# A fused attention and two-expert-stage kernel: 64-bit weight words decoded two tiles at a time, and the first chunk's last four feature blocks computed with split operands

## The chip, the cores and the metric

The kernel runs on one core of one Trainium2 chip. The metric is the device time of one execution in microseconds, the median of three runs.

## What is computed

Three stages follow each other. Windowed attention (4 batches, 8 heads, 576 positions, window 64) gives 2304 rows of 512 numbers. A dense two-layer stage (512 to 2048 to 512) follows, and then a routed stage with 8 experts, where each row goes to one of them. The change touches the dense stage and what is around its start:

```
x = attn_out.transpose(0, 2, 1, 3).reshape(B * S, H * D)     # 2304 x 512
h = x @ w_in                                                 # 512 x 2048
g = where(h >= 1, h, where(h <= -1, 0, (h + 1) ** 2 / 4))
y = g @ w_out                                                # 2048 x 512
# then: expert = argmax(y @ w_gate + bias), out = gate * (relu(y @ w1[e]) @ w2[e])
```

The arrays w_in and w_out reach the device as 64-bit floating-point words, and the kernel turns them into 32-bit numbers itself.

## The kernel before

The rows are worked through in 6 chunks of 384. Within a chunk the loop runs over 16 feature blocks f of 128 columns. For each block, layer 1 (`l1`) multiplies the chunk's x with the block of w_in into a PSUM tile h, ScalarE makes u from it (L456 and L457), VectorE finishes the activation (`act2`, L465), and two steps later (`LAG`) layer 2 (`l2`) multiplies it with the block of w_out and adds into three PSUM tiles py. There are two PSUM tiles h, so `l1` of block f+1 can start only when `act2` of block f-1 has read its h.

TensorE has two ways of doing a product here. With whole 32-bit operands it is 4 matmuls for layer 1 (L436, each recorded as two instructions) and 3 for layer 2 (L483). With split operands, each number is a rounded high part plus a low part, and high times high, high times low and low times high are added: 12 matmuls for layer 1 (L453), 9 for layer 2 (L491). Splitting a weight tile takes a copy on ScalarE (L301) and a subtraction on VectorE (L302). Splitting an activation takes a copy on ScalarE (L473) and a subtraction on VectorE (L474).

In chunk 0 the weights arrive and are decoded step by step, and both layers work on whole operands. A weight tile is [128, 512], and tiles come in pairs p: pair p holds block p-1 of w_out and block p+1 of w_in. Each tile of a pair passes through four kinds of operation: ScalarE takes the magnitude of the upper words (`dec_abs`, L258), VectorE clamps and shifts (`dec_clamp`, L265 and L267), and VectorE merges sign and lower word (`dec_merge`, L273 and L278). In step f, pair f+1 is clamped and merged and pair f+2 gets its magnitudes. Each instruction handles one tile, 512 columns wide, and the two tiles of a pair take turns.

From chunk 1 on, both layers use split operands. The 32 weight tiles are split from the end of chunk 0 into the first half of chunk 1 (`split`). Small copies on GpSimd (`hold_back`, L292) keep the target tiles from being written too early.

The attention of the rows of chunk 1 runs inside the steps of chunk 0: score products on TensorE (L331), the row maximum on VectorE (L346), the exponential on ScalarE (L356), the sum's reciprocal on VectorE (L368, L369), the scaling on ScalarE (L377), the transpose on TensorE (L386), its copy (L391), the product with v (L408) and its split into xh and xl (L428, L429). In chunk 0 every engine's instructions are issued in the order in which `step0` writes them, each engine working strictly through its own row. In chunk 1 a scheduler mixes the engines' rows.

Of the kernel before, what the change touches and what calls it, by code (L numbers as in the profile page):

```python
# [9 lines left out]
F32 = mybir.dt.float32  # L10
F32R = mybir.dt.float32r
# [6 lines left out]
P = 128  # L18
# [53 lines left out]
def moe_kernel(ctx, tc, qT, kT, v, w_in, w_out, mod, wg, wgT, mbias, w1, w2, cst, tri, empty, out, spec):  # L72
# [129 lines left out]
    dec = tile_of([P, 4 * 2 * DM], "dec", I32)  # L202

    PRE = 3

    def part(kind, f, lo):
        return parts[kind, f][0][:, lo * WB : (lo + 1) * WB]

    def raw_home(p, u):
        j = 2 * p + u  # L210
        if j == 2 * NF - 1:
            return dts[p][u]
        if j // 2 not in raws:
# [15 lines left out]
    pairs += [((1, f), (0, f + IN0 - 2)) for f in range(2, NF - IN0 + 2)]  # L229
    pairs += [((1, f), (1, f + 1)) for f in range(NF - IN0 + 2, NF, 2)]  # L230
    NPR = len(pairs)
    dts = {}
# [11 lines left out]
    def words(p, u):  # L244
        w = raw(p, u).rearrange("p (n w) -> p n w", w=2)
        return w[:, :, 0], w[:, :, 1]

    def dec_load(p, us=(0, 1)):
        if p < NPR:
# [3 lines left out]

    def dec_abs(p, us=(0, 1)):
        if p < NPR:
            for u in us:
                dts.setdefault(p, {})[u] = tile_of([P, DM], f"dt{p}_{u}", I32, tag="y", bufs=4)
                A.activation(dts[p][u].bitcast(F32), words(p, u)[1].bitcast(F32), AF.Abs)  # L258

    def dec_clamp(p, us=(0, 1)):  # L260
        if p < NPR:
            t = dts[p]
            for u in us:
                tf = t[u].bitcast(F32)
                V.tensor_scalar(tf, tf, c0, c1, op0=ALU.max, op1=ALU.min)  # L265
            for u in us:
                V.tensor_scalar(t[u], t[u], 5, 2, op0=ALU.logical_shift_left, op1=ALU.logical_shift_right)  # L267

    def dec_merge(p, us=(0, 1)):
        if p < NPR:  # L270
            t = dts[p]
            for u in us:
                V.scalar_tensor_tensor(  # L273
                    t[u], words(p, u)[1], -0x40000000, t[u], op0=ALU.bitwise_and, op1=ALU.bitwise_or
                )
            for u in us:
                w = raw_home(p, u)
                V.scalar_tensor_tensor(  # L278
                    w, words(p, u)[0], 29, t[u], op0=ALU.logical_shift_right, op1=ALU.bitwise_or
                )  # L280
                whole[pairs[p][u]] = w.bitcast(F32)

    whole = {}
    splits = [kf for p in pairs for kf in p]

    def home(k):
        return f"T{NF + k if k < NF else k - NF}"

    def hold_back(g):
        for k in range(len(parts), NF):  # L290
            t = tile_of([P, 2 * WB], f"hold{k}", tag=home(k))
            G.tensor_copy(t[:, :1], g[:, :1])  # L292

# [12 lines left out]

    def new_x(c):
        if c == 0:
            xs[c] = tile_of([P, KD, CT], "x0", tag="xh", bufs=2)
            return  # L310
        xs[c] = tuple(tile_of([P, KD, CT], f"x{s}{c}", F32R, tag=f"x{s}", bufs=2) for s in "hl")

    at, xos = {}, {}
    PAIRED = 2 * BPC
# [102 lines left out]
    def att_x(i):  # L417
        xo = xos.pop(i)
        c, n = divmod(i, BPC)
        dst = slice(n * BLK, (n + 1) * BLK)  # L420
        if i >= PAIRED:
            xos.pop(i + 1)
            dst = slice(n * BLK, n * BLK + GT)
        if c == 0:
            A.copy(xs[c][:, :, dst], xo)
# [7 lines left out]
    def l1_whole(f, g):  # L433
        h = hs[0, f]
        for k in range(KD):
            T.matmul(h[:, g], whole[0, f][:, k * P : (k + 1) * P], xs[0][:, k, g], start=k == 0, stop=k == KD - 1)  # L436

    def l1_tile(t):
        if t == 0:
# [3 lines left out]
    def l1(c, f):  # L443
        if (c, f) not in hs:
            hs[c, f] = ps.tile([P, CT], F32, tag="h", name=f"h{c}_{f}", bufs=2)
            if c == 0:
                l1_whole(f, slice(0, CT))
        h = hs[c, f]
        n = 0
        xh, xl = xs[c] if c else (None, None)  # L450
        for k in range(KD if c else 0):
            for a, b in ((0, xh), (0, xl), (1, xh)):
                T.matmul(h, wi(f, a)[:, k, :], b[:, k, :], start=n == 0, stop=n == 3 * KD - 1)  # L453
                n += 1
        u = tile_of([P, CT], f"u{c}_{f}", tag="u", bufs=2)
        A.activation(u, h, AF.Relu, bias=half, scale=0.5)  # L456
        A.activation(u, u, AF.Square)  # L457
        us[c, f] = u

    def act2(c, f):  # L460
        u, h = us[c, f], hs.pop((c, f))
        g = u
        if c == 0:
            g = gs[c, f] = tile_of([P, CT], f"g{c}_{f}", tag="gh" if f % 2 else "gl", bufs=2)
        V.scalar_tensor_tensor(g, u, 1.0, h, op0=ALU.min, op1=ALU.max)  # L465

    def gsplit(c, f):
        u = us.pop((c, f))
        if c == 0:
            return  # L470
        gh = tile_of([P, CT], f"gh{c}_{f}", F32R, tag="gh", bufs=2)
        gl = tile_of([P, CT], f"gl{c}_{f}", F32R, tag="gl", bufs=2)
        A.copy(gh, u)  # L473
        V.tensor_tensor(gl, u, gh.bitcast(F32), op=ALU.subtract)  # L474
        gs[c, f] = (gh, gl)

    def l2(c, f):
        if f == 0:
            ys[c] = [ps.tile([P, DM], F32, tag=f"y{t}", name=f"py{c}_{t}", bufs=1) for t in range(TT)]
        if c == 0:  # L480
# [491 lines left out]
    def step0(f):  # L972
        if 1 <= f < 4:
            act2(0, f - 1)
        dec_clamp(f + 1)
        dec_merge(f + 1)
        dec_load(f + 4)
        if f >= NF - 2:
            split(2 if f < NF - 1 else 6)
        at_step = {f - st: BPC + k for k, st in enumerate(FIRST)}  # L980
        if 4 in at_step:
            att_pv(at_step[4])
            att_x(at_step[4])
# [175 lines left out]
```

## Time and profile before

| | |
|---|---|
| median of 3 runs | 738.86 us (738.45 to 739.05) |
| the profiled execution, device time | 737.79 us |
| its span, first to last instruction | 736.1 us |
| mean granted TensorE clock | 0.997 of full speed |
| TensorE matmul busy | 723.4 us, 98% |
| VectorE busy | 470.0 us, 64% |
| ScalarE busy | 385.1 us, 52% |
| GpSimd busy | 127.0 us, 17% |

The share of busy time is a mean over stages. Chunk 0 of the dense stage runs from about 20 to 120 us, and chunk 1 from 113 to about 195 us. A matmul's duration in a row includes the time that it spends in the pipeline, so the time from one group of matmuls to the next is read from their starts.

### The profile page before, as it was taken

The numbers are of one execution on the slowest core, as the hardware profiler recorded it, in microseconds if no ns is written. First come the engines' busy times: TensorE is split into PE (matmuls) and PEld (weight loads), VectorE is DVE, ScalarE is ACT, GpSimd is POOL, SyncE is SP. The second block draws the span as 40 slices with busy tenths as digits, with TensorE's granted clock in tenths as the row PEclk, the third lists the DMA queues.
The fourth block names the chain that finished last, engine by engine and source line by source line (L and its number), as shares of the span: only waits on it lengthen the run. The fifth ranks groups of instructions, "written<-read, shape, count | busy, mean of one in ns | idle before, by whom it ended". The sixth has DMA issues, their size and how long they took to land. (4 is left out here: it accounts for less than half of the span.)

```text
span 736.1 us, 12397 instructions
## 1 busy us (share of the span) xinstructions
PE 723.4 (98%) x4168; PEld 617.6 (84%) x4168; DVE 470.0 (64%) x1430; ACT 385.1 (52%) x933; POOL 127.0 (17%) x189
## 2 busy tenths in 40 slices
PE   8999999999999999999999999999999999999995
PEld 6655556888988989898998899899989989898984
DVE  5998889984387528962596638866674554453500
ACT  6775679654455546554555445645434544443511
POOL 3200002012001201120111412032048222201010
PEclk9999999999999999999999999999999999999998
DMA  9986633220022203220310005145456654445300
GB/s 327 334 305 222 245 120 127 91 61 28 32 92 65 80 15 107 73 81 15 108 58 30 2 27 186 60 93 192 161 127 179 220 183 153 158 160 165 119 32 19
DMA packets 48570, 89.26 MB, mean 121 GB/s; under 512 B 6976, under 2 KB 16320, under 8 KB 48368
## 3 DMA queue, kind: packets, MB, share of 16 engines
q1 hardware_dynamic: 44064, 78.36, 32.0%
q0 software_dynamic: 4288, 9.79, 4.9%
q8 instruction: 35, 0.57, 0.3%
q14 instruction: 39, 0.32, 0.1%
q10 hardware_dynamic: 144, 0.22, 0.1%
HBM read 78.89 MB, written 9.87 MB: 121 GB/s over the span
## 5 line engine op out<-in xcount | busy, mean ns | idle before, releaser
L453 PE MATMUL h<-xh,w 128*128 128x384 f32 x640 | 180.0, 342 | 0.4 <-DVE u L465 0.4
L491 PE MATMUL py<-w,gh 128*128 128x512 f32 x480 | 148.6, 393 | 0.0
L453 PEld LDWEIGHTS h<-xh,w 128*128 128x128 f32 x640 | 117.1, 188 | 3.4 <-DVE u L465 0.7
L453 PE MATMUL h<-xl,w 128*128 128x384 f32 x320 | 107.4, 336 | 0.0
L456 ACT ACTIVATE u<-h,half 128x384 f32<-128x384 f32 x96 | 55.4, 577 | 94.6 <-PE h L453 70.8
L737 DVE TENSOR_TENSOR e<-wr,e 128x512 fp32r<-128x512 f32 x112 | 74.6, 689 | 45.3 <-ACT e L736 43.3
L799 PE MATMUL hp<-zh,e 128*128 128x384 f32 x384 | 101.1, 336 | 0.1
L491 PEld LDWEIGHTS py<-w,gh 128*128 128x128 f32 x480 | 88.7, 188 | 14.6
L814 PE MATMUL yo<-e,hm 128*128 128x512 f32 x348 | 99.0, 395 | 0.0
L491 PE MATMUL py<-w,gl 128*128 128x512 f32 x240 | 94.0, 397 | 0.0
L465 DVE SCALAR_TENSOR_TENSOR u<-u,h 128x384 f32<-128x384 f32 x80 | 44.0, 550 | 74.0 <-ACT u L457 73.7
L545 DVE CUSTOM_DVE_ANT_0 prod<-y,wgb 128x512 f32<-128x512 f32 x120 | 85.1, 709 | 1.2
L473 ACT CAST gh<-u 128x384 fp32r<-128x384 f32 x80 | 41.1, 513 | 73.2 <-PE py L491 29.7
L814 PEld LDWEIGHTS yo<-e,hm 128*128 128x128 f32 x348 | 64.2, 188 | 12.4
L736 ACT CAST e<-wr 128x512 fp32r<-128x512 f32 x112 | 66.2, 616 | 16.2 <-DMA wr<-in_w 16.0
L799 PEld LDWEIGHTS hp<-zh,e 128*128 128x128 f32 x384 | 69.7, 188 | 1.3 <-DVE hm L802 0.6
L379 POOL TENSOR_TENSOR s<-s,sm 128x512 f32<-128x512 f32 (+1 forms) x24 | 26.3, 1096 | 234.0 <-DVE sm L369 166.9
L799 PE MATMUL hp<-zl,e 128*128 128x384 f32 x192 | 64.3, 335 | 0.0
L453 PEld LDWEIGHTS h<-xl,w 128*128 128x128 f32 x320 | 60.2, 188 | 2.3 <-issue 0.2
L474 DVE TENSOR_TENSOR gl<-u,gh 128x384 fp32r<-128x384 f32 x80 | 44.9, 561 | 26.9 <-ACT gh L473 26.1
L491 PEld LDWEIGHTS py<-w,gl 128*128 128x128 f32 x240 | 44.8, 188 | 9.5
L356 ACT ACTIVATE s<-s,mx 128x128 f32<-128x128 f32 (+1 forms) x120 | 45.9, 384 | 13.1 <-DVE mx L346 13.1
(209 smaller groups left out, 1054.8 us busy)
## 6 DMA issues: line engine op xcount, KB each, us to landing
wr<-in_w SPq DMA_DIRECT2D x112, 256.0 KB, 2.9
q<-in_qT SPq DMA_DIRECT2D x32, 256.0 KB, 3.6
dec<-in_w_in SPq DMA_DIRECT2D x16, 512.0 KB, 5.2
dec<-in_w_out SPq DMA_DIRECT2D x16, 512.0 KB, 4.0
v<-in_v SPq DMA_DIRECT2D x27, 256.0 KB, 2.9
k<-in_kT SPq DMA_DIRECT2D x15, 384.0 KB, 4.7
yd<-y SPq DMA_DIRECT2D x18, 256.0 KB, 2.2
wgb<-in_wgT SPq DMA_DIRECT2D x1, 2048.0 KB, 7.4
```

The source lines that it names most:

```text
L356: A.activation(s[:, hp, :n], s[:, hp, :n], AF.Exp, bias=mx[:, hp : hp + 1], scale=-1.0, accum_out=sm[:, hp : hp + 1],)
L453: T.matmul(h, wi(f, a)[:, k, :], b[:, k, :], start=n == 0, stop=n == 3 * KD - 1)
L456: A.activation(u, h, AF.Relu, bias=half, scale=0.5)
L465: V.scalar_tensor_tensor(g, u, 1.0, h, op0=ALU.min, op1=ALU.max)
L473: A.copy(gh, u)
L474: V.tensor_tensor(gl, u, gh.bitcast(F32), op=ALU.subtract)
L491: T.matmul(ys[c][t], a[:, sl], wo(f, b), start=f == 0 and n == 0, stop=f == NF - 1 and n == 2)
L545: V.tensor_tensor_reduce(prod, yt[t], wgb[0][:, e, :], 1.0, 0.0, ALU.mult, ALU.add, lg[:, t, e : e + 1])
L736: A.copy(wpart(i, p, 0), t)
L737: V.tensor_tensor(wpart(i, p, 1), t, wpart(i, p, 0).bitcast(F32), op=ALU.subtract)
L799: T.matmul(hp, w1s(i, f, k, a), b[:, k, :], start=n == 0, stop=n == 3 * KD - 1)
L814: T.matmul(yo, a[f][:, sl], w2s(i, f, b), start=n == 0, stop=n == 3 * NF2 - 1)
```

## The change

Two things are changed.

First, the decoding handles both tiles of a pair with one instruction where the pair's words lie next to each other (two pairs of three): magnitudes, clamp, shift and merges are then 1024 columns wide. In the third pair of three only clamp and shift are. The pair's intermediate tile moves from four half-size buffers into two full-size ones.

Second, the blocks 12 to 15 of chunk 0 use split operands in layer 1 and in layer 2. For this, x of chunk 0 is split in two halves (`split_x0`, in steps 8 and 9), the weight tiles concerned are split within steps 11 to 15 (`split_hi` at the end of a step on ScalarE, `split_lo` at the start of the next on VectorE, ahead of that step's decoding), and the activations of blocks 12 to 15 are split (`gsplit`, called in `step0` ahead of `dec_abs`). The number of weight splits stays 32: ten lie in chunk 0, 22 in chunk 1.

```diff
+    soon = {f: [(0, f + 1)] for f in range(FS1 - 1, NF - 1)}
+    for f in range(FS2, NF - 1):
+        soon.setdefault(f + 1, []).append((1, f))
+    soon[NF - 1] += [(0, 0), (0, 1), (1, NF - 1)]
...
     def dec_clamp(p, us=(0, 1)):
         if p < NPR:
-            t = dts[p]
-            for u in us:
-                tf = t[u].bitcast(F32)
-                V.tensor_scalar(tf, tf, c0, c1, op0=ALU.max, op1=ALU.min)
-            for u in us:
-                V.tensor_scalar(t[u], t[u], 5, 2, op0=ALU.logical_shift_left, op1=ALU.logical_shift_right)
+            t = dts[p][:, us[0] : us[-1] + 1]
+            V.tensor_scalar(t.bitcast(F32), t.bitcast(F32), c0, c1, op0=ALU.max, op1=ALU.min)
+            V.tensor_scalar(t, t, 5, 2, op0=ALU.logical_shift_left, op1=ALU.logical_shift_right)
...
+    def split_hi(kf):
+        tag = free.pop(0)
+        t = tile_of([P, 2 * WB], f"w{kf[0]}_{kf[1]}", F32R, tag=tag)
+        w = whole.pop(kf)
+        A.copy(t[:, :WB], w)
+        halves.append((kf, t, tag, w))
+
+    def split_lo():
+        kf, t, tag, w = halves.pop(0)
+        V.tensor_tensor(t[:, WB:], w, t[:, :WB].bitcast(F32), op=ALU.subtract)
...
     def step0(f):
         if 1 <= f < 4:
             act2(0, f - 1)
+        if f == NF - 1:
+            free.extend(f"T{NF + k}" for k in (14, 15, 8, 9))
+        for kf in soon.get(f, []):
+            split_lo()
         dec_clamp(f + 1)
         dec_merge(f + 1)
         dec_load(f + 4)
-        if f >= NF - 2:
-            split(2 if f < NF - 1 else 6)
+        if f in (FS1 - 4, FS1 - 3):
+            split_x0(f - FS1 + 4)
...
         l1(0, f)
         if f >= 4:
             act2(0, f - 1)
+            gsplit(0, f - 1)
+        else:
+            us.pop((0, f - 1), None)
         dec_abs(f + 2)
...
         if f >= LAG:
             l2(0, f - LAG)
+        for kf in soon.get(f + 1, []):
+            split_hi(kf)
```

Where the instructions stand now is shown at three places. The first is VectorE at step 12 of chunk 0, before. dt13 is the intermediate of pair 13, raw13 its decoded tiles, g0_11 the finished activation of block 11, sm11 the sum of an attention block.

```order
L265 TENSOR_SCALAR dt13_0_979<-dt13_0_979 128x512
L265 TENSOR_SCALAR dt13_1_981<-dt13_1_981 128x512
L267 TENSOR_SCALAR dt13_0_979<-dt13_0_979 128x512
L267 TENSOR_SCALAR dt13_1_981<-dt13_1_981 128x512
L273 SCALAR_TENSOR_TENSOR dt13_0_979<-dec_106,dt13_0_979 128x512
L273 SCALAR_TENSOR_TENSOR dt13_1_981<-dec_106,dt13_1_981 128x512
L278 SCALAR_TENSOR_TENSOR raw13_1003<-dec_106,dt13_0_979 128x512
L278 SCALAR_TENSOR_TENSOR raw13_1003<-dec_106,dt13_1_981 128x512
L465 SCALAR_TENSOR_TENSOR g0_11_1021<-u0_11_974,h0_11_969 128x384
```

The same place on VectorE now; w0_13 is the split tile of block 13 of w_in.

```order
L320 TENSOR_TENSOR w0_13_946<-raw12_893,w0_13_946 128x512
L274 TENSOR_SCALAR dt13_930<-dt13_930 128x1024
L275 TENSOR_SCALAR dt13_930<-dt13_930 128x1024
L281 SCALAR_TENSOR_TENSOR dt13_930<-dec_106,dt13_930 128x1024
L294 SCALAR_TENSOR_TENSOR raw13_951<-dec_106,dt13_930 128x1024
L508 SCALAR_TENSOR_TENSOR g0_11_977<-u0_11_925,h0_11_920 128x384
```

Eight instructions of 512 columns have become four of 1024, each working on what the one ahead of it wrote, and the weight's low part stands ahead of all of them.

The second place is ScalarE at the end of step 11, before. u0_11 is block 11's activation, s11 an attention block, ts10 a copied transpose.

```order
L456 ACTIVATE u0_11_974<-h0_11_969,half_78 128x384
L457 ACTIVATE u0_11_974<-u0_11_974 128x384
L258 ACTIVATE dt13_0_979<-dec_106 128x512
L258 ACTIVATE dt13_1_981<-dec_106 128x512
L356 ACTIVATE s11_983,sm11_989<-s11_983,mx11_984 128x128 x4
L391 COPY ts10_1011<-pt10_1006 128x512
```

The same place on ScalarE now.

```order
L499 ACTIVATE u0_11_925<-h0_11_920,half_78 128x384
L500 ACTIVATE u0_11_925<-u0_11_925 128x384
L269 ACTIVATE dt13_930<-dec_106 128x1024
L398 ACTIVATE s11_932,sm11_938<-s11_932,mx11_933 128x128 x4
L315 CAST w0_13_946<-raw12_893 128x512
L433 COPY ts10_959<-pt10_954 128x512
```

The copy that VectorE's first instruction of step 12 works on stands behind the four exponentials.

The third place is ScalarE in steps 12 to 14, now: the scaling of s11 (which uses the reciprocal sm11 that VectorE computes behind g0_11), and the activation's high part gh0_12.

```order
L269 ACTIVATE dt14_979<-dec14_1_858 128x512
L419 ACTIVATE s11_932<-s11_932,sm11_938 128x128 x4
L315 CAST w0_14_991<-raw13_951 128x512
L315 CAST w1_12_993<-raw13_951 128x512
L470 CAST xh1_424<-xo10_1004 128x4x64
L499 ACTIVATE u0_13_1028<-h0_13_1015,half_78 128x384
L500 ACTIVATE u0_13_1028<-u0_13_1028 128x384
L516 CAST gh0_12_1032<-u0_12_974 128x384
L269 ACTIVATE dt15_1036<-dec_106 128x1024
L315 CAST w0_15_1041<-raw14_999 128x512
L315 CAST w1_13_1043<-raw14_999 128x512
```

Before, the same stretch holds the scaling, the activations and the two magnitudes of dt15, without the five copies L315 and L516.

```order
L258 ACTIVATE dt14_1_1025<-dec14_1_906 128x512
L377 ACTIVATE s11_983<-s11_983,sm11_989 128x128 x4
L428 CAST xh1_427<-xo10_1045 128x4x64
L456 ACTIVATE u0_13_1061<-h0_13_1056,half_78 128x384
L457 ACTIVATE u0_13_1061<-u0_13_1061 128x384
L258 ACTIVATE dt15_0_1066<-dec_106 128x512
L258 ACTIVATE dt15_1_1068<-dec_106 128x512
```

The copies of the weights now stand behind the scaling in one step, and behind gh0_12 and the magnitudes in the next.

## Rows read from the trace of the kernel before

**Rows 1.** Busy time of each engine in one stretch: PE, PEld, DVE, ACT, POOL, clock, DMA.

```profile
100.00:120.00 20.00, 20.00 (x95) 13.17 (x94) 19.73 (x49) 16.88 (x39) 2.55 (x8) 1.00 0.50 178
```

**Rows 2.** TensorE's timeline in chunk 0: start, duration, line, operation, tiles, count.

```profile
82.34 1.16 PE L331 MATMUL sc<-k,q 128*128 128x128 f32 x8
...
85.92 2.74 PE L483 MATMUL py<-raw,g 128*128 128x512 f32 x6
88.50 0.60 PE L386 MATMUL pt<-cs,s 128*128 128x128 f32 x4
88.93 2.75 PE L436 MATMUL h<-x,raw 128*128 128x384 f32 x8
91.52 2.74 PE L483 MATMUL py<-raw,g 128*128 128x512 f32 x6
94.18 0.69 PE L408 MATMUL xo<-ts,v 128*64 128x64 f32 x16
94.80 2.85 PE L436 MATMUL h<-x,raw 128*128 128x384 f32 x8
```

**Rows 3.** VectorE's timeline in steps 11 and 12 of chunk 0.

```profile
85.78 0.28 DVE L346 CUSTOM_DVE_ANT_0 s<-sc,cs 128x128 f32<-128x128 f32 x1
...
87.85 1.00 DVE L265 TENSOR_SCALAR dt<-dt 128x512 f32<-128x512 f32 x2 [1.15 <-ACT dt L258]
...
89.44 1.28 DVE L273 SCALAR_TENSOR_TENSOR dt<-dec,dt 128x512 int32<-128x512 int32 x2
...
91.85 0.54 DVE L465 SCALAR_TENSOR_TENSOR g<-u,h 128x384 f32<-128x384 f32 x1
...
92.50 0.18 DVE L369 RECIPROCAL sm<-sm 128x4 f32<-128x4 f32 x1
```

**Rows 4.** TensorE's timeline in a later chunk, where operands are split.

```profile
302.04 0.63 PE L491 MATMUL py<-w,gh 128*128 128x512 f32 x2
...
304.12 0.33 PE L453 MATMUL h<-xh,w 128*128 128x384 f32 x1
...
306.22 0.63 PE L491 MATMUL py<-w,gh 128*128 128x512 f32 x2
```

**Rows 5.** VectorE's timeline where one tile alone is decoded.

```profile
20.59 0.43 DVE L267 TENSOR_SCALAR dt<-dt 128x512 int32<-128x512 int32 x1
...
21.05 0.69 DVE L273 SCALAR_TENSOR_TENSOR dt<-dec,dt 128x512 int32<-128x512 int32 x1
...
21.78 0.69 DVE L278 SCALAR_TENSOR_TENSOR raw<-dec,dt 128x512 int32<-128x512 int32 x1
```

**Rows 6.** Timeline of ScalarE, VectorE and TensorE's weight loads in steps 0 to 2.

```profile
22.50 0.68 ACT L258 ACTIVATE dt<-dec 128x512 f32<-128x512 f32 x1
...
26.63 0.55 DVE L465 SCALAR_TENSOR_TENSOR g<-u,h 128x384 f32<-128x384 f32 x1
...
27.24 2.37 PEld L436 LDWEIGHTS h<-x,raw 128*128 128x128 f32 x8 [0.21 <-DVE g L465]
```

**Rows 7.** ScalarE's timeline in steps 11 and 12 of chunk 0.

```profile
86.12 0.58 ACT L456 ACTIVATE u<-h,half 128x384 f32<-128x384 f32 x1 [3.17 <-PE h L436]
...
89.84 0.56 ACT L391 COPY ts<-pt 128x512 f32<-128x512 f32 x1
...
93.88 1.27 ACT L377 ACTIVATE s<-s,sm 128x128 f32<-128x128 f32 x4
```

**Rows 8.** Groups by line (busy us, mean ns), and rows around the start of chunk 1.

```profile
L302 DVE TENSOR_TENSOR w<-raw,w 128x512 fp32r<-128x512 f32 x31 | 20.6, 712 | 0.5 <-ACT w L301 0.5
L301 ACT CAST w<-raw 128x512 fp32r<-128x512 f32 x31 | 17.3, 613 | 1.2 <-POOL hold L292 1.2
...
110.68 1.89 DVE L302 TENSOR_TENSOR w<-raw,w 128x512 fp32r<-128x512 f32 x3
...
123.58 0.42 PEld L386 LDWEIGHTS pt<-cs,s 128*128 128x128 f32 x4 [1.52 <-POOL s L379]
```

**Rows 9.** Busy time of each engine and granted clock after TensorE's last matmul.

```profile
730.00:733.00 3.00, 0.00 (x0) 0.00 (x0) 0.00 (x0) 0.00 (x0) 0.08 (x1) 0.73 0.06 17
```

More of the change, by code (lines that the diff above doesn't have):

```diff
@@ L231, in moe_kernel @@
     NPR = len(pairs)
+    soon = {f: [(0, f + 1)] for f in range(FS1 - 1, NF - 1)}
+    for f in range(FS2, NF - 1):
+        soon.setdefault(f + 1, []).append((1, f))
+    soon[NF - 1] += [(0, 0), (0, 1), (1, NF - 1)]
+    later = [kf for kfs in pairs for kf in kfs if kf not in sum(soon.values(), [])]
+    lone_kf = later[-1]
     dts = {}
@@ L242, in raw, with words @@
         return dec[:, o : o + 2 * DM]
-    def words(p, u):
-        w = raw(p, u).rearrange("p (n w) -> p n w", w=2)
-        return w[:, :, 0], w[:, :, 1]
+    def words(p, us):
+        if p % 3 < 2 and len(us) == 2:
+            o = p % 3 * 4 * DM
+            both = dec[:, o : o + 4 * DM].rearrange("p (u n w) -> p u n w", u=2, w=2)
+            return [(both[:, :, :, 0], both[:, :, :, 1], slice(0, 2))]
+        each = [(u, raw(p, u).rearrange("p (u n w) -> p u n w", u=1, w=2)) for u in us]
+        return [(w[:, :, :, 0], w[:, :, :, 1], slice(u, u + 1)) for u, w in each]
     def dec_load(p, us=(0, 1)):
@@ L269, in dec_merge @@
     def dec_merge(p, us=(0, 1)):
         if p < NPR:
-            t = dts[p]
-            for u in us:
+            t, r = dts[p], raw_home(p)
+            for _, top, u in words(p, us):
                 V.scalar_tensor_tensor(
-                    t[u], words(p, u)[1], -0x40000000, t[u], op0=ALU.bitwise_and, op1=ALU.bitwise_or
+                    t[:, u], top, -0x40000000, t[:, u], op0=ALU.bitwise_and, op1=ALU.bitwise_or
                 )
[L276 to L281, printed above, removed]
+            for low, _, u in words(p, us):
+                outs = [(u, r[:, u])]
+                if lone_kf in pairs[p]:
+                    lone = tile_of([P, 1, WB], "lone", I32, tag="y", bufs=4)
+                    outs = [
+                        (slice(v, v + 1), lone if pairs[p][v] == lone_kf else r[:, v : v + 1])
+                        for v in range(u.start, u.stop)
+                    ]
+                for v, o in outs:
+                    q = slice(v.start - u.start, v.stop - u.start)
+                    V.scalar_tensor_tensor(
+                        o, low[:, q], 29, t[:, v], op0=ALU.logical_shift_right, op1=ALU.bitwise_or
+                    )
+                    for k in range(v.start, v.stop):
+                        whole[pairs[p][k]] = o[:, k - v.start].bitcast(F32)
@@ L283, in moe_kernel @@
     whole = {}
-    splits = [kf for p in pairs for kf in p]
-    def home(k):
-        return f"T{NF + k if k < NF else k - NF}"
+    pair_of = {kf: p for p, kfs in enumerate(pairs) for kf in kfs}
+    left = {p: sum(kf != lone_kf for kf in kfs) for p, kfs in enumerate(pairs)}
+    free = [f"T{NF + k}" for k in (0, 1, 2, 3, 4, 5, 6, 7, 12, 13)]
+    halves = []
     def hold_back(g):
-        for k in range(len(parts), NF):
-            t = tile_of([P, 2 * WB], f"hold{k}", tag=home(k))
+        for tag in free:
+            t = tile_of([P, 2 * WB], f"hold{tag}", tag=tag)
@@ L305, in moe_kernel @@
+    def split_lo():
+        kf, t, tag, w = halves.pop(0)
+        V.tensor_tensor(t[:, WB:], w, t[:, :WB].bitcast(F32), op=ALU.subtract)
+        parts[kf] = (t, tag)
+        if kf != lone_kf:
+            p = pair_of[kf]
+            left[p] -= 1
+            if not left[p]:
+                free.append(f"T{p}")
+    def split(n):
+        for kf in later[:n]:
+            split_hi(kf)
+            split_lo()
+        del later[:n]
     xs = {}
@@ L308, in new_x, with split_x0 @@
         if c == 0:
-            xs[c] = tile_of([P, KD, CT], "x0", tag="xh", bufs=2)
+            whole_x.append(tile_of([P, KD, CT], "x0", tag="xh", bufs=2))
             return
         xs[c] = tuple(tile_of([P, KD, CT], f"x{s}{c}", F32R, tag=f"x{s}", bufs=2) for s in "hl")
+    whole_x = []
+    KH = KD // 2
+    def split_x0(j):
+        if not j:
+            hi = [tile_of([P, 2 * WB], f"x0h{n}", F32R, tag=f"T{NF + 10 + n}") for n in range(2)]
+            hi = [t[:, : KH * CT].rearrange("p (k n) -> p k n", k=KH) for t in hi]
+            xs[0] = (hi, tile_of([P, KD, CT], "x0l", F32R, tag="xl", bufs=2))
+        hi, lo = xs[0]
+        ks = slice(j * KH, (j + 1) * KH)
+        A.copy(hi[j], whole_x[0][:, ks])
+        V.tensor_tensor(lo[:, ks], whole_x[0][:, ks], hi[j].bitcast(F32), op=ALU.subtract)
     at, xos = {}, {}
@@ L424, in att_x @@
         if c == 0:
-            A.copy(xs[c][:, :, dst], xo)
+            A.copy(whole_x[0][:, :, dst], xo)
             return
@@ L435, in l1_whole @@
         for k in range(KD):
-            T.matmul(h[:, g], whole[0, f][:, k * P : (k + 1) * P], xs[0][:, k, g], start=k == 0, stop=k == KD - 1)
+            T.matmul(h[:, g], whole[0, f][:, k * P : (k + 1) * P], whole_x[0][:, k, g], start=k == 0, stop=k == KD - 1)
     def l1_tile(t):
@@ L449, in l1 @@
         n = 0
[L450 to L453, printed above, removed]
+        for k in range(KD if c or f >= FS1 else 0):
+            xh, xl = xs[c]
+            xh = xh[:, k, :] if c else xh[k // KH][:, k % KH, :]
+            for a, b in ((0, xh), (0, xl[:, k, :]), (1, xh)):
+                T.matmul(h, wi(f, a)[:, k, :], b, start=n == 0, stop=n == 3 * KD - 1)
                 n += 1
@@ L468, in gsplit @@
         u = us.pop((c, f))
-        if c == 0:
+        if c == 0 and f < FS2:
             return
```

45 lines of the change are left out of this document (19 added, 26 removed).

## The prediction

> **What bounds the kernel now.** I read the busy time of each engine by stretches first, then the timelines of TensorE, VectorE and ScalarE side by side in the steps that change. By the stretches TensorE is the bound: it is busy for all 20 us of the stretch in which the changed steps lie, at full clock [rows 1]. A microsecond taken off TensorE would therefore come off the end. But the same row says that VectorE is busy for 19.73 of those 20 us and ScalarE for 16.88, so VectorE has almost nothing to spare, and whatever the change adds there has to be followed. The timelines show how the two are tied. `l1` of a block reuses the PSUM tile that `act2` of the block two before has to read first, and `act2` stands in VectorE's row behind the whole decoding of its step. Before, `l1` of block 13 starts at 94.80 [rows 2], and `act2` of block 11 ends at 91.85 + 0.54 = 92.39 [rows 3]. That cover of 2.4 us is what hides VectorE now.
>
> **What the split operands take off TensorE.** Layer 1 of a block takes 91.52 - 88.93 = 2.59 us with whole operands, layer 2 takes 88.50 - 85.92 = 2.58 [rows 2]. With split operands the same products take 306.22 - 304.12 = 2.10 and 304.12 - 302.04 = 2.08 [rows 4]. Four blocks of both give 4 x 0.49 + 4 x 0.50 = 4.0 us. No other TensorE work is added or removed. Term: **-4.0** (bounds -3.3 to -4.2, as the pipelines fit together).
>
> **What pairing does to the decoding.** The two tiles of a pair take turns now, so each instruction starts while the one ahead, which works on the other tile, is still in the pipeline: two merges take 1.28 us together [rows 3], where one alone has 0.69 [rows 5]. The second costs 0.59. In the new order each instruction needs the result of the one right ahead. Where the trace has such a chain, the next starts only after the end: 20.59 to 21.05 is 0.46 for a shift of 0.43, 21.05 to 21.78 is 0.73 for a merge of 0.69 [rows 5]. A merge of 1024 columns I take as 0.69 + 0.55 + 0.03, about 1.26; a clamp or shift as 0.75 (bounds: 0.46, if the second half cost nothing, and 0.89, if it cost its full 0.43). The chain is then 2 x 0.75 + 2 x 1.26 less 0.1 at its end, 3.9 us, against 91.85 - 87.85 = 4.0 now [rows 3]. So 49 decoding instructions fewer on VectorE gain nothing that I can see in a step.
>
> The Trainium skill, page Perfetto Trace Analysis, section Optimizing Scalar/DVE Operations, puts a cost of about 60 ns on each VectorE instruction in SBUF and says that grouping into larger ones helps a saturated engine. It would make the chain about 0.25 us shorter than the halves; the rows agree on the cost, but show that turn-taking already hides it. This is a rival below.
>
> At the very start there is a price. The second tile's magnitudes of pair 1 start at 22.50, the first's earlier; one instruction for both must wait for the later place and then takes some 0.4 us longer, and the chain behind it loses its overlap, another 0.4. `act2` of block 0, at 26.63, moves by that, and the weight load of `l1` of block 2 already waits 0.21 us for it [rows 6], so there is no cover. Term: **+0.8** (0.3 to 1.3).
>
> **The wait ahead of block 13.** Count from the start of block 11's activation on ScalarE, 86.12 [rows 7]. Now the first clamp of step 12 starts at 87.85, 1.7 us later [rows 3]. In the new order VectorE's first instruction there is the low part of w0_13, which needs a copy that ScalarE makes behind the four exponentials. These end where the copy of ts10 starts, 89.84 - 86.12 = 3.7; the copy takes 0.61 [rows 8], one wide magnitude saves about 0.1, so VectorE starts at 4.2. Then come 0.60 for the low part, 3.9 for the chain and 0.57 for `act2`: 9.3. TensorE reaches `l1` of block 13 at 94.80 - 86.12 = 8.7 now [rows 2], and 0.5 earlier with block 12 split: 8.2. Term: **+1.1** (0.3 to 1.8).
>
> **The wait ahead of block 14.** Count from that `act2`'s end. VectorE computes the reciprocal (92.50 + 0.18 - 92.39 = 0.3), ScalarE does the scaling that needs it (1.27 [rows 7]) and behind it the copy of w0_14 (0.61): with the handovers, 2.2 us in which VectorE stands still. Then two low parts 1.2, clamp and shift 1.5, four narrow merges 2.4, xl 0.4, `act2` 0.57: 8.2 in all. TensorE has 2.10 + 2.58 and a transpose of 88.93 - 88.50 = 0.43 to do [rows 2, 4]: 5.1. Term: **+3.0** (2.0 to 3.6).
>
> **The wait ahead of block 15.** From the next `act2`'s end, ScalarE first makes gh0_12, then the magnitudes of pair 15, then the copy of w0_15: 0.5 + 1.0 + 0.61, VectorE starts at 2.2. Two low parts 1.2, clamp and shift 1.5, a merge 1.26, four maxima of the next attention block (0.28 each at most [rows 3], 0.9), the last merge 1.2, `act2` 0.57: 8.7. TensorE has 2.10 + 2.08, the product with v 0.62 (94.80 - 94.18) and two score products of about 1.05 (the row's 1.16 has the last one's way through the pipeline in it) [rows 2, 4]: 6.9. Term: **+1.8** (0.8 to 2.4).
>
> **Chunk 1's start.** Thirteen of the 32 low parts are issued ahead of chunk 1's first `l1` now, the last three from 110.68 on [rows 8]; in the new order it is ten, and two activation splits are added behind it. That is 3 x 0.60 + 2 x 0.5, near 2.8 us more on VectorE (the group's mean of 712 ns has each one's pipeline in it [rows 8]), in a stretch where VectorE is full and where TensorE already waits, as the load at 123.58 shows with 1.52 us [rows 8]. TensorE's work there is shorter by the 1.0 already counted, so it arrives earlier still. I take **+2.3**, between 0 (the waits of before cover it) and 4 (it adds on to them, and the copies queue on ScalarE too). GpSimd's holds, eleven instead of eight, and the two splits of x0 (steps 8 and 9) I cost at nothing: the cover of 2.4 us is whole in those steps; without it each split of x0 would cost about 0.9. SP's row is unchanged, and each load is asked for behind the same merge.
>
> **The sum.** -4.0 + 0.8 + 1.1 + 3.0 + 1.8 + 2.3 = +5.0 us. After chunk 1 TensorE is again the bound and gives nothing back. The profiled execution took 737.79 us, 1.7 of it outside its span; that gives 742.8. It is 1.1 us under the median of the runs, so for the median I forecast **743.9**.
>
> **Rival A, VectorE stays covered (faster).** If the 2.4 us of cover hold, only the -4.0 is left: 734.9. The point that decides is the place of w0_13's low part: `l1` of block 13 does not wait if VectorE starts step 12 before 3.1 (8.2 - 5.1) after 86.12's event, and block 14 not if its 2.2 us of standstill and 0.8 more vanish. For it: TensorE never idles in this stretch today. Against it: the copy's place behind the exponentials, and 19.73 of 20 [rows 1]. Chance 0.08.
>
> **Rival B, pairing pays.** If the second half of a clamp or shift costs nothing (0.46 instead of 0.75, the lower bound above), each chain is about 0.5 us shorter. The three waits then fall by 0.5 each, the start's price to near nothing, chunk 1 by 0.5: 5.0 - 2.8 = +2.2, 741.1. Chance 0.15. The page named above points this way.
>
> **Rival C, the clock falls.** In the stretch after TensorE's last matmul the granted clock's mean is 0.73 [rows 9], so an idle TensorE falls from 2.4 to 1.2 GHz. If the 3 us ahead of block 14 do this, the matmuls behind it run at half speed, and one `l1` and half of an `l2` more is 3 us: 746.9. Against it: no row of the work itself shows a lower clock, though none has so long a wait. Chance 0.10. The Trainium skill, page TensorE: Matmul & The Clock Gate, Part 1, says that an idle array falls to the lower level; the trace agrees at the end of the span, and shows nothing of a shorter idle time.
>
> **How the numbers follow.** The forecast has 0.67, A 0.08, B 0.15, C 0.10. The bounds of the terms add to -0.8 and +9.8; taken as independent they leave about 2.5 us either way, which gives 741.4 to 746.4. To take in B and C the range is **740.6 to 747.0**. A measurement of this kernel can tell about 0.2%, 1.5 us, from no change: faster by more than that 0.08 (A), slower 0.84 (forecast, C, most of B), the same 0.08 (the low ends of B and of the forecast).
>
> **What would show it.** In the new profile, timeline of TensorE: layer 1 of blocks 12 to 15 near 2.1 us, and idle time ahead of the first matmul of blocks 13, 14 and 15, released by VectorE's `act2`, longest at 14. VectorE should idle ahead of the low parts, released by ScalarE's copies, some 1.7, 1.7 and 1.1 us. The wide merge should take 1.2 us and start after the end of the one ahead. If TensorE shows no idle time in 85 to 120 us, the forecast is wrong by A; if the wide clamp takes 0.5 us, by B; a clock under 1.00 there is C. If the three waits are there, but the time differs, chunk 1's start is the term that was mis-sized.

## The result: 0.9% slower, most of it for the reasons given

The changed kernel takes 745.79 us (median of 6, 744.34 to 746.83), the kernel before 738.95 in the same comparison: ratio 1.0091, 95% interval 1.0077 to 1.0106, or +6.8 us. The forecast was 743.9, with a range of 740.6 to 747.0. The profiled execution took 745.06 us, with a span of 743.3.

Busy time by stretches of the changed kernel (columns as in [rows 1]):

```profile
100.00:120.00 20.00, 15.18 (x90) 11.87 (x88) 17.98 (x43) 12.62 (x36) 1.31 (x1) 1.00 0.24 92
```

TensorE, busy for all 20 us of 100 to 120 before, is idle for 4.8 of them now, and VectorE is not busier but less busy: 17.98 against 19.73 [rows 1]. Both stand still for a part of the time. TensorE's timeline (start, duration; in brackets the idle time ahead and what ended it) has these waits at the start, and these ahead of blocks 13, 14, 15 and of chunk 1's first `l1`. The rows at 90.74 and 92.91 are the starts of block 12's `l1` and of the `l2` behind it:

```profile
28.74 2.85 PE L478 MATMUL h<-x,raw 128*128 128x384 f32 x8 [0.50 <-DVE g L508]
...
90.74 0.42 PE L496 MATMUL h<-x0h,w 128*128 128x384 f32 x1
...
92.91 1.45 PE L526 MATMUL py<-raw,g 128*128 128x512 f32 x3
...
97.94 0.45 PE L496 MATMUL h<-x0h,w 128*128 128x384 f32 x1 [1.68 <-DVE g L508]
...
106.13 0.41 PE L496 MATMUL h<-x0h,w 128*128 128x384 f32 x1 [2.83 <-DVE u L508]
...
114.86 0.44 PE L496 MATMUL h<-x0h,w 128*128 128x384 f32 x1 [1.73 <-DVE u L508]
...
120.46 0.41 PE L496 MATMUL h<-xh,w 128*128 128x384 f32 x1 [0.72 <-DVE sm L410]
```

A second short wait of 0.26 us stands ahead of block 5. Layer 1 of block 12 takes 92.91 - 90.74 = 2.17 us, where it took 2.59 [rows 2]. So TensorE's gain is there and is waited away. In chunk 1 there are four more waits:

```profile
135.83 1.66 PE L534 MATMUL py<-w,gh 128*128 128x512 f32 x6 [1.01 <-ACT gh L516]
138.24 0.45 PE L496 MATMUL h<-xh,w 128*128 128x384 f32 x1 [0.75 <-DVE u L508]
...
143.25 0.96 PE L534 MATMUL py<-w,gl 128*128 128x512 f32 x3 [0.58 <-DVE gl L517]
144.99 0.45 PE L496 MATMUL h<-xh,w 128*128 128x384 f32 x1 [0.78 <-DVE u L508]
```

VectorE's timeline in steps 11 to 14 shows where it stands still itself, each time ahead of a low part (L320), released by ScalarE's copy:

```profile
85.02 0.69 DVE L320 TENSOR_TENSOR w<-raw,w 128x512 fp32r<-128x512 f32 x1 [2.39 <-ACT w L315]
...
92.87 0.69 DVE L320 TENSOR_TENSOR w<-raw,w 128x512 fp32r<-128x512 f32 x1 [1.60 <-ACT w L315]
93.48 0.69 DVE L274 TENSOR_SCALAR dt<-dt 128x1024 f32<-128x1024 f32 x1
94.20 0.69 DVE L275 TENSOR_SCALAR dt<-dt 128x1024 int32<-128x1024 int32 x1
94.93 1.23 DVE L281 SCALAR_TENSOR_TENSOR dt<-dec,dt 128x1024 int32<-128x1024 int32 x1
96.19 1.23 DVE L294 SCALAR_TENSOR_TENSOR raw<-dec,dt 128x1024 int32<-128x1024 int32 x1
97.33 0.55 DVE L508 SCALAR_TENSOR_TENSOR g<-u,h 128x384 f32<-128x384 f32 x1
...
97.99 0.18 DVE L411 RECIPROCAL sm<-sm 128x4 f32<-128x4 f32 x1
...
100.03 1.29 DVE L320 TENSOR_TENSOR w<-raw,w 128x512 fp32r<-128x512 f32 x2 [1.86 <-ACT w L315]
...
108.11 1.29 DVE L320 TENSOR_TENSOR w<-raw,w 128x512 fp32r<-128x512 f32 x2 [0.99 <-ACT w L315]
...
110.77 1.23 DVE L281 SCALAR_TENSOR_TENSOR dt<-dec,dt 128x1024 int32<-128x1024 int32 x1
112.28 0.29 DVE L388 CUSTOM_DVE_ANT_0 s<-sc,cs 128x128 f32<-128x128 f32 x1 [0.28 <-PE sc L373]
...
113.13 1.22 DVE L294 SCALAR_TENSOR_TENSOR raw<-dec,dt 128x1024 int32<-128x1024 int32 x1
114.27 0.55 DVE L508 SCALAR_TENSOR_TENSOR u<-u,h 128x384 f32<-128x384 f32 x1
```

The last four rows are the end of step 14: four row maxima (L388) stand between the pair's two merges, ahead of `act2` of block 13 at 114.27. ScalarE's timeline at the same places shows why the copies (L315) come late: the exponentials wait for VectorE's maxima, the scaling for its reciprocal, and the copy stands behind them.

```profile
88.01 0.58 ACT L499 ACTIVATE u<-h,half 128x384 f32<-128x384 f32 x1 [2.75 <-PE h L478]
...
90.67 0.40 ACT L398 ACTIVATE s<-s,mx 128x128 f32<-128x128 f32 x1 [0.47 <-DVE mx L388]
...
92.23 0.60 ACT L315 CAST w<-raw 128x512 fp32r<-128x512 f32 x1
...
98.21 1.28 ACT L419 ACTIVATE s<-s,sm 128x128 f32<-128x128 f32 x4 [2.70 <-DVE sm L411]
99.40 1.12 ACT L315 CAST w<-raw 128x512 fp32r<-128x512 f32 x2
```

This is a circle. VectorE waits for ScalarE's copy, the copy for the scaling, the scaling for the reciprocal, and that stands behind an `act2` that VectorE issues late since it waited for the copy before.

**Where the 6.8 us are.** I count starts of `l1` from each profile's first one (20.41 before, 21.01 after), so that the 0.6 us by which the first starts differ stay out. In the eight experiments it lies between 20.34 and 20.98, in no order that I can see. Start and shift count from there; the cost of the waits is that of the row's own interval, the growth of the shift with TensorE's saving (0.49 for each split `l1`, 0.50 for each split `l2` in it) added back.

| up to the start of | before | after | shift | cost of the waits | forecast |
|---|---|---|---|---|---|
| block 12 | 68.52 | 69.73 | +1.21 | 1.2 | 0.8 |
| block 13 | 74.39 | 76.93 | +2.54 | 1.8 | 1.1 |
| block 14 | 80.09 | 85.12 | +5.03 | 3.0 | 3.0 |
| chunk 1 | 92.91 | 99.45 | +6.54 | 3.1 | 1.8 for block 15, |
| chunk 2 | 173.85 | 180.57 | +6.72 | 1.6 | 2.3 for chunk 1 |
| sum | | | | 10.7 | 9.0 |

Less 4.0 that is 6.7 against 5.0. (Ahead of chunk 1's first `l1` four transposes of 0.43 in all now stand that stood behind it; the two last rows are corrected for them.)

### The profile page after: what moved, and what is told of

Same layout as the page of the kernel before. It is cut to its first block, busy times and chain, and to the rows that moved or that the text cites. A ratio compares the mean times of both kernels' runs of the same rounds, so it can differ in the third digit from the quotient of the medians.

```text
span 743.3 us, 12397 instructions
## 1 busy us (share of the span) xinstructions
PE 720.2 (97%) x4196; PEld 621.8 (84%) x4196; DVE 474.1 (64%) x1387; ACT 387.5 (52%) x929; POOL 126.1 (17%) x192
## 5 line engine op out<-in xcount | busy, mean ns | idle before, releaser
L534 PE MATMUL py<-w,gh 128*128 128x512 f32 x504 | 155.8, 393 | 1.0 <-ACT gh L516 1.0
L534 PEld LDWEIGHTS py<-w,gh 128*128 128x128 f32 x504 | 93.0, 188 | 16.8 <-ACT gh L516 1.3
L534 PE MATMUL py<-w,gl 128*128 128x512 f32 x252 | 98.2, 396 | 0.6 <-DVE gl L517 0.6
L508 DVE SCALAR_TENSOR_TENSOR u<-u,h 128x384 f32<-128x384 f32 x84 | 46.3, 551 | 75.0 <-ACT u L500 74.7
L516 ACT CAST gh<-u 128x384 fp32r<-128x384 f32 x84 | 43.1, 514 | 75.7 <-DVE u L508 32.6
L517 DVE TENSOR_TENSOR gl<-u,gh 128x384 fp32r<-128x384 f32 x84 | 48.3, 576 | 27.5 <-ACT gh L516 26.6
L534 PEld LDWEIGHTS py<-w,gl 128*128 128x128 f32 x252 | 47.1, 188 | 10.8 <-DVE gl L517 1.0
```

What stands on the lines that cost most here:

```text
L534: T.matmul(ys[c][t], a[:, sl], wo(f, b), start=f == 0 and n == 0, stop=f == NF - 1 and n == 2)
```

## The experiments

My theory: the low parts' place at the head of VectorE's step, with the copies behind attention work on ScalarE, costs what is lost in steps 11 to 15, and the pairing brings nothing. Rivals: pairing pays by itself; or the added work is too much for VectorE wherever it stands. Ratios are to the kernel before on the same chip (738.56 us for the first four runs, 738.99 for the others).

| run | us | ratio (95%) | waits of TensorE at blocks 2 and 5; 13, 14, 15 |
|---|---|---|---|
| changed kernel | 745.79 | 1.0091 (1.0077 to 1.0106) | 0.50, 0.26; 1.68, 2.83, 1.73 |
| pairs alone | 741.53 | 1.0046 (1.0031 to 1.0061) | 0.49, 0.26; none |
| split alone | 741.38 | 1.0038 (1.0024 to 1.0051) | none; 1.48, 2.71, none |
| lows on GpSimd | 739.60 | 1.0015 (1.0005 to 1.0024) | 0.49, 0.26; none, 1.26, 0.87 |
| lows late | 735.56 | 0.9961 (0.9948 to 0.9974) | 0.49, 0.26; none |
| lows late, halves | 734.04 | 0.9930 (0.9915 to 0.9945) | none |
| copies early | 742.98 | 1.0057 (1.0038 to 1.0076) | 0.50, 0.27; none, 0.39, 1.73 |
| lows late, pair 1 in halves | 735.21 | 0.9946 (0.9928 to 0.9964) | none |
| lows late, halves, from block 11 | 734.14 | 0.9932 (0.9917 to 0.9948) | none |

**Pairs alone.** The wide decoding, with whole operands in all of chunk 0 and the weight splits called where the kernel before has them:

```diff
-    FS1, FS2 = 12, 12
+    FS1, FS2 = NF, NF
...
-        if f in (FS1 - 4, FS1 - 3):
-            split_x0(f - FS1 + 4)
+        if f >= NF - 2:
+            split(2 if f < NF - 1 else 6)
```

> Decoding by pairs alone; chunk 0 stays with whole operands and its weight splits stand where they stood before. Theory (a wide instruction costs what two turn-taking ones cost, and the start of block 2 is held up): 1 to 2 us slower than before, about 740.5, with an idle time of about 0.5 us ahead of layer 1 of block 2 and none ahead of blocks 12 to 15. Rival (pairing takes 49 fixed costs off VectorE and pays): 738 or less. If pairing is what costs the 6.8 us: 744 or more.

It is 3.0 us slower than before, more than the 1 to 2 expected: pairing doesn't pay, it costs. The start's two waits are the changed kernel's own, and `l1` of block 11 starts 1.28 us later than before, counted from the first. In chunk 1 TensorE's waits grow from 1.1 us to 2.1, the longest of them 1.55 us at 127.92, released by VectorE. In the trace chunk 2 starts 2.3 us later than before; what makes up the rest of the 3.0 is not followed. Here the Trainium skill (Perfetto Trace Analysis, Optimizing Scalar/DVE Operations) has a second sentence, which the prediction did not weigh: where VectorE is not saturated but leaves TensorE idle, breaking instructions up may let work complete sooner. The trace agrees with that one, by 0.5 us at block 2.

**Split alone.** The split operands as in the change, the decoding in halves that take turns (`WIDE_WORDS` is False; magnitudes and shift are cut up in the same way as the clamp shown):

```diff
-        if p % 3 < 2 and len(us) == 2:
+        if WIDE_WORDS and p % 3 < 2 and len(us) == 2:
...
-            t = dts[p][:, us[0] : us[-1] + 1]
-            V.tensor_scalar(t.bitcast(F32), t.bitcast(F32), c0, c1, op0=ALU.max, op1=ALU.min)
+            ts = [dts[p][:, u : u + 1] for u in us]
+            for t in ts:
+                V.tensor_scalar(t.bitcast(F32), t.bitcast(F32), c0, c1, op0=ALU.max, op1=ALU.min)
...
```

> Split operands in blocks 12 to 15 alone; the decoding takes turns in halves as before. Theory (the low parts in front of VectorE's row and ScalarE's copies behind other work hold up act2): waits ahead of blocks 13, 14 and 15 of about 1.3, 2.5 and 1.2 us, none ahead of block 2, 4 to 5 us slower than before, about 743.5. Rival (the waits come from the longer chain of wide instructions): the waits are mostly gone and the time is 737 or less.

It is 2.8 us slower than before, where 4 to 5 were expected, with the waits ahead of blocks 13 and 14 almost as in the changed kernel and none at the start. With the 3.0 of the pairs that is 5.8 of the 6.8. The wait ahead of block 15 isn't there, for two reasons. The four maxima of step 14 belong to chunk 1's part of the program, which a scheduler orders, and in this run they stand behind `act2` of block 13. So it ends 7.58 us behind block 14's start, where in the changed kernel it ends 8.69 behind. The other reason is TensorE's clock, told in the last section.

**Lows on GpSimd.** VectorE is relieved of the low parts of steps 11 to 14:

```diff
-    def split_lo():
+    def split_lo(eng=V):
...
-        V.tensor_tensor(t[:, WB:], w, t[:, :WB].bitcast(F32), op=ALU.subtract)
+        eng.tensor_tensor(t[:, WB:], w, t[:, :WB].bitcast(F32), op=ALU.subtract)
...
-            split_lo()
+            split_lo(G if f < NF - 1 else V)
```

> The changed kernel, with the low parts of the weights of steps 11 to 14 (six of the ten) computed on GpSimd, which is idle there, instead of VectorE. Theory: VectorE no longer stands still for ScalarE's copies nor does the work, the three waits fall from 6.2 us to under 1, and the time to about 739 (737.5 to 741). Rival (TensorE waits for the split weights or for ScalarE's copies themselves): the waits stay, or grow because GpSimd takes longer for a tile than VectorE's 0.69 us, 745 or more.

Most of the loss goes, but waits ahead of blocks 14 and 15 are left, 2.1 us in all where under 1 was expected. The timelines of GpSimd and VectorE in step 13 show why (the first fence is GpSimd, the second VectorE):

```profile
97.24 2.96 POOL L320 TENSOR_TENSOR w<-raw,w 128x512 fp32r<-128x512 f32 x2 [3.75 <-ACT w L315]
```

```profile
96.67 2.40 DVE L281 SCALAR_TENSOR_TENSOR dt<-dec,dt 128x512 int32<-128x512 int32 x2
...
101.27 0.41 DVE L471 TENSOR_TENSOR xl<-xo,xh 128x256 fp32r<-128x256 f32 x1
```

While GpSimd subtracts, VectorE's four merges take 101.27 - 96.67 = 4.6 us. In the next run, with GpSimd idle there, they take 98.61 - 96.20 = 2.4. Two low parts taken from VectorE (1.2 us) cost it 2.2.

**Lows late.** The same instructions on the same engines; VectorE only issues the low parts behind `act2` instead of ahead of the decoding:

```diff
-        for kf in soon.get(f, []):
-            split_lo()
         dec_clamp(f + 1)
...
             act2(0, f - 1)
+            for kf in soon.get(f, []):
+                split_lo()
             gsplit(0, f - 1)
```

> The changed kernel, with the same low parts on VectorE, but behind the step's decoding and act2 instead of ahead of them. The work on every engine is the same. Theory (the place in VectorE's row, ahead of the decoding, is what costs): the waits ahead of blocks 13 to 15 go to under 1 us in all, about 738.5 (736.5 to 741). Rival (VectorE has simply too much work in these steps, wherever it stands): the waits stay in sum, 744 or more.

The move is worth about 10 us against the changed kernel, and the kernel is now 0.39% faster than before, just outside the expected range of 736.5 to 741. VectorE's timeline from the end of step 12 to step 14:

```profile
93.41 0.55 DVE L508 SCALAR_TENSOR_TENSOR g<-u,h 128x384 f32<-128x384 f32 x1
93.88 0.68 DVE L320 TENSOR_TENSOR w<-raw,w 128x512 fp32r<-128x512 f32 x1
...
94.77 0.67 DVE L274 TENSOR_SCALAR dt<-dt 128x1024 f32<-128x1024 f32 x1
...
96.20 1.29 DVE L281 SCALAR_TENSOR_TENSOR dt<-dec,dt 128x512 int32<-128x512 int32 x2
...
98.61 0.42 DVE L471 TENSOR_TENSOR xl<-xo,xh 128x256 fp32r<-128x256 f32 x1
...
103.88 1.22 DVE L294 SCALAR_TENSOR_TENSOR raw<-dec,dt 128x1024 int32<-128x1024 int32 x1
105.03 0.55 DVE L508 SCALAR_TENSOR_TENSOR u<-u,h 128x384 f32<-128x384 f32 x1
...
106.84 0.29 DVE L388 CUSTOM_DVE_ANT_0 s<-sc,cs 128x128 f32<-128x128 f32 x1
```

No low part has idle time ahead of it, since its copy has long been made, and in step 13 the next decoding starts at once. With that the rival "too much work wherever it stands" falls: all of it fits. The circle is broken here.

One thing moved along with the low parts: the scheduler puts the four maxima of step 14 behind `act2` here too (106.84). In the changed kernel they and the idle time ahead of them put off the last merge by about 113.13 - 112.00 = 1.1 us, so up to 1.1 of the 1.73 us ahead of block 15 may be theirs. In the steps ahead of blocks 13 and 14 the two rows differ in nothing but the low parts.

**Copies early.** The other place to break it: ScalarE's copies ahead of the exponentials and the scaling, the low parts left where the change put them.

```diff
         dec_abs(f + 2)
+        for kf in soon.get(f + 1, []):
+            split_hi(kf)
...
-        for kf in soon.get(f + 1, []):
-            split_hi(kf)
```

> The changed kernel with one thing moved: ScalarE makes the copies of the weights (the high parts) right behind the magnitudes, ahead of the exponentials and the scaling. The low parts stay at the head of VectorE's step. Theory (VectorE stands still for the copy, and the copy for what ScalarE does ahead of it): the standstill ahead of the low part of w0_13 falls by the exponentials, from 1.6 us to under 0.4, that of w0_14 by the scaling and its wait, from 1.9 to under 0.6; the one of w0_15 stays near 1.0, since nothing stands between its magnitudes and its copy now. TensorE's wait ahead of block 13 is then 0 to 0.4 (was 1.68), ahead of block 14 0.6 to 1.3 (was 2.83), ahead of block 15 1.4 to 2.0 (was 1.73): 3 us less in all, ratio 1.004 to 1.007, about 742 us. Rival (the low parts' and chains' own time on VectorE is what costs, wherever the copies stand): the waits keep over 5 us in all, ratio 1.008 or above.

VectorE's low parts in steps 11 to 14 of this run:

```profile
83.59 0.69 DVE L320 TENSOR_TENSOR w<-raw,w 128x512 fp32r<-128x512 f32 x1 [1.24 <-ACT w L315]
...
90.46 0.69 DVE L320 TENSOR_TENSOR w<-raw,w 128x512 fp32r<-128x512 f32 x1 [0.62 <-ACT w L315]
...
95.69 1.30 DVE L320 TENSOR_TENSOR w<-raw,w 128x512 fp32r<-128x512 f32 x2
...
103.78 0.69 DVE L320 TENSOR_TENSOR w<-raw,w 128x512 fp32r<-128x512 f32 x1 [0.99 <-ACT w L315]
```

The standstills fall from 2.39, 1.60, 1.86 and 0.99 us to 1.24, 0.62, none and 0.99: the three whose copy had stood behind exponentials or scaling fall, and the last, whose copy never did, not at all. The waits ahead of blocks 13 to 15 fall from 6.24 to 2.12 us. Only 2.8 of these 4.1 us reach the end. A new wait of 3.94 us opens in chunk 1, where ScalarE copies a transpose behind a row of weight copies, and the clock falls in it (last section).

**Lows late, halves.** As "lows late", with the decoding in halves as in "split alone".

> The split operands of blocks 12 to 15 stay, each weight's low part is computed behind act2 (as in the run with late lows), and the decoding is done in halves that take turns, as before the change, everywhere. Theory (the place of the low parts cost what the changed kernel lost in steps 12 to 14, and the pairing itself costs its dependent chains, with no gain anywhere): only TensorE's saving of 4.0 us is left, no wait at blocks 2, 5, 13, 14 and 15, time ratio to the kernel before 0.9940 to 0.9955, some 734.5 us; against the run with late lows and pairs (735.56) about 1.0 us less. Rival (pairing helps once VectorE's row is in the right order, since it issues 49 instructions fewer): halves are no faster than the pairs there, ratio 0.9961 or above, and a wait comes back ahead of block 13, 14 or 15 or at chunk 1's start.

734.04 us, the fastest measured: 0.70% under the kernel before, 11.75 us under the changed one. In the trace chunk 2 starts 4.65 us earlier than before, counted from the first `l1`; 4.0 was expected. Of the 4.65, 2.83 are there when chunk 1 starts, where 3.0 were due, and 1.82 come within chunk 1, where 1.0 was due. TensorE's idle time in chunk 1 is about the same (1.02 us, 1.11 before), so the 0.8 too many are not waits saved; where they come from I have not followed. Pairs bring nothing in the right order either: by the ratios the run with them is 0.3% slower.

**Lows late, pair 1 in halves.** As "lows late"; only pair 1 is decoded in halves, its first tile's magnitudes early:

```diff
-        if p % 3 < 2 and len(us) == 2:
+        if p != 1 and p % 3 < 2 and len(us) == 2:
...
+    dec_abs(1, (0,))
     l1_tile(0)
...
-    dec_abs(1)
+    dec_abs(1, (1,))
```

> The run with late lows, and pair 1 alone decoded in halves with its first tile's magnitudes early, as before the change; all other pairs stay wide. Theory (the price at the start is the chain of pair 1, whose wide instructions cannot begin on the first tile): the wait ahead of block 2 (0.5 us) goes. If the wait ahead of block 5 (0.26) is what block 2's delay left, it goes too and 0.8 to 1.3 us are gained, ratio 0.9943 to 0.9950; if it belongs to the wide chain of pair 4, it stays at 0.2 to 0.5 and 0.5 to 0.8 are gained, ratio 0.9950 to 0.9955. Rival (the start's later first matmul is chance and pair 1 costs nothing): ratio 0.9961 as with late lows and pairs.

Both waits at the start go, and block 5 starts 1.0 us earlier against the first `l1` than with all pairs (25.74 and 26.75 us; 25.57 before). So the wait at block 5 was mostly what block 2's delay left. By the ratios the gain is 0.15%, 1.1 us, though the intervals overlap.

**Lows late, halves, from block 11.** As "lows late, halves", with `FS1, FS2 = 11, 11`.

> Late lows and decoding in halves everywhere, and one block more with split operands: 11 to 15. Theory (TensorE is the bound as long as each act2 comes in time): 1.0 us less on TensorE, two weight splits more in chunk 0 and two fewer in chunk 1, one activation split more; with no new wait the ratio is 0.9925 to 0.9942, some 733.5 us. Rival (VectorE's 4 us of spare time per 20 are used up by the added split of an activation and two low parts a step): the waits come back ahead of blocks 12 to 15, 0.5 us or more in all, and the time is that of the run with blocks 12 to 15, or above.

No difference from blocks 12 to 15 that can be told, so the theory's 1.0 us did not come. The rival's waits ahead of blocks 12 to 15 did not come either. In the trace 0.69 us are gained when chunk 1 starts and 0.34 when chunk 2 does. In chunk 1 there is a new wait:

```profile
139.67 0.50 PE L538 MATMUL py<-w,gl 128*128 128x512 f32 x1 [0.65 <-DVE gl L521]
```

But the waits of chunk 1 sum up to no more than in that run (0.97 us, there 1.02), so what takes the gain is not shown.

## Why the prediction was right, and where its terms were off

**TensorE, -4.0: held.** "Lows late, halves" has the same products and no wait in these steps, and gains 4.65 us in its trace, 2.83 of them by the start of chunk 1, when 3.0 of the 4.0 were due.

**Pairing gains nothing: held.** The chain of step 12 takes 97.33 - 93.48 = 3.85 us (forecast 3.9). A wide merge starts 96.19 - 94.93 = 1.26 after the one ahead (forecast 1.26), a wide clamp 0.72 (forecast 0.75). "Pairs alone" shows a loss. Rival B fell. One sentence of the prediction goes too far: that its rows agree with the fixed cost of an instruction. None of them separates it; the runs come nearer, with 1.28 us for two merges that take turns and 1.23 for a wide one.

**The start, +0.8: mechanism right, size low.** The wait ahead of block 2 costs what was forecast: block 3 starts 0.77 us later against the first `l1`. Missed was the wait ahead of block 5, another 0.4 (1.21 up to block 12 in all). I looked for a cover only at block 2.

**Block 13, +1.1: measured 1.8.** I let the exponentials end 3.7 us after the start of block 11's activation, as before. They now end 92.23 - 88.01 = 4.2 after it, since their first waits 0.47 us for VectorE's maxima, and these are late because of a standstill that the prediction left out: the low part of w0_12 at the head of step 11, 2.39 us. I had taken the 2.4 us of cover for enough there. It was, for TensorE; it was not for the next step's own inputs.

**Block 14, +3.0: measured 3.0.** Standstill forecast 1.7, measured 1.86; wait 2.83. The parts that the prediction lists for VectorE add up to 8.27 here and to 8.83 for block 15, where it has 8.2 and 8.7; the two terms would be about 0.1 larger each.

**Block 15 and chunk 1, +1.8 and +2.3: measured 4.7 together, and for chunk 1 the number came out by luck.** Standstill ahead of block 15 forecast 1.1, measured 0.99; wait 1.73. In chunk 1 the waits grew from 1.1 us (0.69 and 0.42 before) to 3.8. The prediction put this down to the low parts and activation splits that now stand behind chunk 1's start. But "lows late, halves" has just as many of them there, ten low parts ahead of the start and 22 behind, and its waits in chunk 1 are 1.02 us. So this work by itself does not make TensorE wait. The pairs alone bring 1.0 of the growth; what brings the rest is open.

**Rival A** fell: TensorE waits at every place named. "Lows late" shows that its mechanism was only one place in a row away, and its time of 734.9 is near what that kernel takes (735.56).

**Rival C** did not come in the profiled execution, with a granted clock of 1.00 in the stretches shown above. But in "split alone" the clock did fall behind the wait ahead of block 14, and the price was misjudged; see below.

## What to carry to other kernels

An added instruction that waits for another engine belongs behind the work that a third engine is waiting for, not at the head of the row: here the same instructions cost about 10 us in one place, and in the other TensorE did not wait for them. Before merging two instructions into a wider one, look whether they take turns with others in the pipeline; merged into a dependent chain, they save no time and only start later. When a wait is added that has cover, follow what else stands behind it on that engine, because the delay can come round through a second engine and meet the next step without cover.

## What the runs showed of the hardware

**GpSimd holds VectorE up.** While GpSimd ran two subtractions (2.96 us), VectorE's merges, which read two tiles as well, took about twice their time (4.6 us against 2.4). One step on, a shift that reads one tile took 1.68 us in place of 0.69. The rows look like taking turns rather than a slower VectorE: a merge at 91.12, under way when GpSimd began at 91.76, took its usual 1.23 us, and the one behind it, at 92.38, took 2.19, which is 0.97 longer; GpSimd's subtraction ended 1.10 after that merge's start. The Trainium skill (Perfetto Trace Analysis, Optimizing Scalar/DVE Operations) says that the two engines share an SBUF read port, so that moving work between them might not help; the trace agrees, and here it cost VectorE more than the work taken away.

**After a wait of 2.71 us TensorE's clock fell, and half of what that cost was hidden.** In the changed kernel's profile the wait of 2.83 us left the granted clock at 1.00. In "split alone" a wait of 2.71 us at the same place, ended at 104.37, was followed by this (columns as in [rows 1]):

```profile
104.00:105.00 1.00, 0.63 (x4) 0.66 (x5) 0.42 (x2) 0.74 (x2) 0.00 (x0) 1.00 0.00 0
105.00:106.00 1.00, 1.00 (x6) 1.00 (x5) 0.36 (x1) 1.00 (x3) 0.00 (x0) 0.81 0.00 0
106.00:107.00 1.00, 1.00 (x5) 1.00 (x5) 0.56 (x1) 1.00 (x3) 0.00 (x0) 0.50 0.00 0
...
108.00:109.00 1.00, 1.00 (x3) 0.71 (x3) 1.00 (x5) 0.64 (x2) 0.00 (x0) 0.50 0.00 0
109.00:110.00 1.00, 1.00 (x6) 0.78 (x4) 1.00 (x3) 0.00 (x0) 0.00 (x0) 0.98 0.03 8
```

The clock stood at 0.50 (1.2 GHz) up to 109, with TensorE busy again. These are the rows of TensorE and, in the second fence, `act2` of block 13 on VectorE, which block 15 needs:

```profile
104.37 0.41 PE L500 MATMUL h<-x0h,w 128*128 128x384 f32 x1 [2.71 <-DVE u L512]
...
107.29 1.05 PE L538 MATMUL py<-w,gh 128*128 128x512 f32 x2
...
110.28 0.69 PE L454 MATMUL xo<-ts,v 128*64 128x64 f32 x16
...
112.70 0.42 PE L500 MATMUL h<-x0h,w 128*128 128x384 f32 x1
```

```profile
111.40 0.55 DVE L512 SCALAR_TENSOR_TENSOR u<-u,h 128x384 f32<-128x384 f32 x1
```

Layer 1 of block 14 took 107.29 - 104.37 = 2.92 us from start to start and the layer 2 behind it 110.28 - 107.29 = 2.99, where the changed kernel's took 2.16 and 2.18: 1.57 us more. `act2` ends at 111.40 + 0.55 = 111.95, and block 15 starts 0.75 later, without a wait. At the full clock TensorE would have been there at about 111.1 and would have waited 0.8 us for `act2` (an estimate from these rows). So about half of the price filled a wait, and the other half put block 15 off; whether that half reaches the end is not shown. Rival C took the price for 3 us and added all of it to the waits.

In "copies early" the clock fell within the wait itself. TensorE was idle from 125.7 to 129.7:

```profile
126.00:128.00 2.00, 0.00 (x0) 0.00 (x0) 2.00 (x5) 2.00 (x5) 0.00 (x0) 0.89 0.00 0
128.00:130.00 2.00, 0.32 (x6) 0.33 (x8) 2.00 (x6) 2.00 (x6) 0.00 (x0) 0.50 0.70 259
```

Waits of 2.83, 2.71 and 3.94 us gave three answers, so these runs don't say what decides it. The Trainium skill (TensorE: Matmul & The Clock Gate, Part 1) says that an idle array falls to the lower level; the trace agrees at 3.94 us, and shows no fall at 2.83. The mean clock of the changed kernel's other executions lies between 0.993 and 0.996, that of the profiled one at 0.997, so it may have fallen in some of them; no trace of those was taken.
